# Six full products ahead of a searched run of row-tiled matmuls, with a new table of the run

## The chip, the cores and the metric

One core of a Trainium2 chip runs the whole kernel in one launch. The metric is the device time of one execution in microseconds; the number given for a kernel is the median of its runs. Less is better.

## What is computed

A cross network of six layers over 16,384 rows of 416 features, in bf16:

```python
def reference(x0, ws, bs):
    x = x0
    L = ws.shape[0]
    for l in range(L):
        proj = jnp.einsum('bd,de->be', x, ws[l]) + bs[l]
        x = x0 * proj + x
    return x
```

`x0` is 16384 x 416, `ws` 6 x 416 x 416, `bs` 6 x 416.

## The kernel before

**Tiles.** The batch is cut into 8 groups of 2,048 rows (columns on the chip, since x is held transposed: features on the 128 partitions). A pair (g, l) of group and layer is a job; there are 48. A group's columns are four chunks of 512. The 416 features are three blocks of 128 and a rest of 32. So a job has three output tiles (i = 0, 1, 2) of four chunks each, and a "tail", the 32 output features that are left, for which all four chunks share one bank.

A chunk of an output tile is a sum over 416 inputs, that is three input tiles of 128 (t = 0, 1, 2) and the rest of 32, in one PSUM bank. It can be made in two ways. As *full* products (function `full`, L694), one per input tile, with all 128 rows of the array, and one of 32 rows for the rest. Or as thirteen products of 32 rows each (L1153 for the input tiles, L1157 for the rest): three per row group and one more in the row group that holds the rest. Products in different row groups run side by side, so four of them do what a full one does, but the odd one of the thirteen can be packed with others. Two row groups must not work on the same bank at the same time, so a chunk goes from row group to row group.

**What follows a chunk.** ACT reads the bank, adds the bias and writes `tw` (L595); DVE multiplies a pair of chunks by x0 (L607) and adds x (L615). Tails are made in batches of three (L741 and L729) and evacuated by ACT and DVE (L661, L657, L663, L665). Some tails need their residual rotated by partition quarters, which SP does with DMAs (L487, L488). Outputs are transposed by DMA (L945, L957, and L952 for tails), the tails are spread into the rows by a copy (L980, on POOL, and once, for group 5, on DVE), and the rows are stored (L987, L1003).

**The order.** The first jobs are written out by hand, with full products. From the second tile of job (0, 2) on, `stream` emits 528 chunks as 32-row products only (524 searched ones and four that begin the last output). Their order comes from the string `ORDER`, found by a search beforehand. Each letter takes one chunk (named by its age among those begun) to one row group and runs all its products there; "|" stands for a batch of tails, at which all row groups stop. `replay` steps through the string with a clock of its own: a product takes 20 units (`SLOT`), going to another row group of the same bank costs `FENCE`, a batch of tails costs 60 units per tail and `PHASE`; ACT's reading and the sums of the level below give due times (`READ`, `NEXT`, `BACK`, `SUMS`). `banks` lists when the eight banks are free at the run's start, and `act` when ACT is. The engines don't follow that clock: only the order and the choice of banks are taken from it, and semaphores do the waiting. Instructions on SP, ACT, DVE and POOL are issued in order, each in the order in which `stream` recorded them.

In `replay` before, each of the first four chunks has three products per row group like all others, and the start values are

```python
    free, flight, begun, act = [0] * 4, {}, 0, 156
    banks = [(0, 0), (0, 1), (0, 2), (0, 3), (84, 4), (84, 5), (178, 6), (178, 7)]
```

After the run the last output, group 7's last layer, is made in its natural layout (L1218, evacuated by ACT L1267, multiplied and added by DVE L1273 and L1279, stored by L1286).

Of the kernel before, what the change touches and what calls it, by code (L numbers as in the profile page):

```python
# [5 lines left out]
T32 = 32  # L6
# [15 lines left out]
class Program:  # L22
# [192 lines left out]
ORDER = (  # L215
    "ABCDMBCTZOELBaAjZSIfFiQPVKHYBCcTVIDSJATKBQLWBQXKNALCZQLWBQCbMRLWBITWBQPCZMLWRALSBQLCRIbCRAPeJYWH"
    "N|AWPJQGDQBDWNITCJnQCZTIWBLQWNALWBQXCNIDWZIDWJYTCRbIWBLQBSbINWHAVCTUBOQLBaTARaDQZOLUSBDUORbICJbA"
    "aVTMGBPYBWPIRaHAORDYKBXQKBTIWBDUOZITCZIOTFADeRYPCNIbWQFPK|ABPWAVKPQBCPQVKDAVePQBKfMRaHJAbSIBKTAZ"
    "SLcNHCBQXBSMLBaAOXZQKHMVSDBQOXBMKXAVKDQVKDBMebUJOHAVObIRCLQBSfJ|EODBTAOZACbVcPKFAeXRYGPBYWPRAKPQ"
    "BiLMRGDNACbNAaXNISHBYCTNYCbVISPFAePBUKDVQaDRIOXFAOXBAObVQGLBcCXNAePZIWTFASPBcKPRUGDNAWDNQXCJAbWR"  # L220
    "APSJYDaRUDSJUfOF|ITCRIODJAbSJATJCQDOBPcWJDIeVbQOFXAVODUKBXQKBTIBaLQCZTAOQZLWFPAWNDUCNTUBOTIBaLQN"
    "WALVCQXBOQLBaTINWDIVODUCNXAOJXAWJDUeYBXOIZHSUBTOIBbCMZDWIZTO|EBPWQBOLAVCPQVKfMFSDARWPANXCUNSDIBS"
    "XYBTKAReLMVSbIBKTAhSLYNHCBQXNCMLWBAaPQVKDQBaPBUKjMZSXEBSPAZKPQVHCBQWDMRKXBIWDVAOXJAWfYJTCQZOLEBW"
    "DcRCTMJWbERKP|ABPWQBKPAVCPQVKDANebUBKXQNaHJASXIBKTAhSLYNHCBQXNCMLWBAaXQNKHAZWTMBKDYRKXNAWDNQXBOQ"
    "BObIRWDQBOTICfZAXaRIPFCYPBaUPCMVaLBIWDVQCPRICfJAebJUSPFAaPQVGL|MBDSNAPKBAObRUGLBAeXNYKHVAWTJAKTY"
    "BLCYRWDRIOXBIWPBUOLRAKbBAWPZQCLRYCbNIWTBISPBYKPRAeDQVPKAJXCURCPQJaDIBafQVGPBMaXRIOH|ABTOAZKPQBKD"
    "BUPaAVKbQdCbMRWLEBWTARKPYBWDNQKDZISXBIOTBAOfRYKDZQLWBQKXARKXMBWLBQCPZAWbJQGDQZWPBIWPQBOLAVCPQVKj"
    "MFSDARWPANXCUNSLEBSDYRCTIBafIVOTE|BPWRALOBcDOZQKXBIDVaITCRIbBSYLBSIXNaALVOQDKBQXKBITBaQLVOADOZXA"
    "WJAXSJYDSJYXOFQDZOAXBOQXBOQLBaITVCQDSZMLWBIXSBQLOBIbCZQLCZITWBQLBaITNWALVCUTBSATNaIDJWYTBSPAdOXY"
    "SF|AODVPAKNYXCBQXaJcHORAPaRIHCBUbCRMLWBIWTBQKPVALWRMGDBQCbRMWLBAWbNAKPZUCXQJaPBIWPBcKPVAWLMRCLBQ"  # L230
    "XCRMLWFAWTBQCPZAaPJAWbJMSDZcPCNXYSF|AOTBPAaBYSPJUGDdQODJMbWBIXOdAXKNQHCBQWDMRCbJAaTVIODJAfaUBXSc"
    "NKHAZSXIBLCVYLSNEXCMBWPIBWLAVCXQBOTAdaPUBOLQVaHJAbCMZSLUBSLARKfARWLMBKDYRCPRIbWBQXJOALBaQVCPISXB"
    "ASPYVKHMBCbNQeDJMSXZIP|FCATBaQPBOIDaVIDSJYDSZMXGJTASBjMCNULCVITBeQLNWADaRXMCJDYSBQPaJAbWRAjSJUPG"
    "dQLOBAPSBYPCVIPSBIDSVYDKRAbeJMXGBXMCVIPSBcLORALiNAXOJQDCNUTBOAXBeQPaBYLOVALWdMTGBYfSVMLG|ABWPAVK"
    "PQBCPVQCPJAebVAWLNQaHBYOXBUOLAVKbMRGDBQWDMRKXAJCbQVOLEBaXABOTYVGLMRWDIBSXIBTKAZSLMBKDQZKXARWDQNX"
    "KBISXNADOBcWbBMSXIZGDRYCTZIWPBIWfNQGLB|AWPRAKPBUCPRUKDJAbeJQPWFICXBUPChMLWFAWTBQKPVAWLNQCLBQCbMR"
    "WDJMWDVISPFAObBUCPVQKfNALWBQWLNACbRMLCYJTWARLW|AJTMWDJUCTVICTJWADVaMTBaNIDKVYTOBAfaNQLVGMTCJMSDA"
    "BXa"
)


def replay(tails, events, needs, keep):
# [27 lines left out]
    for letter in ORDER:  # L270
        if letter == "|":
# [13 lines left out]
            for k, (_, b) in enumerate(got):  # L285
# [32 lines left out]
def bass_standalone__cross_network_dcn__recsys_kernel(  # L318
# [8 lines left out]
    NT = 3  # L327
    NJ = 4
# [15 lines left out]
    n = 0  # L344
# [678 lines left out]
    items = []  # L1023
# [85 lines left out]
    def stream(run):  # L1109

        chunks, due = [], []
# [20 lines left out]
        count, seen, natural = {}, {}, {}  # L1132
        for _, r, c, b in plan:
            if r < 0:
                dve[0] = max(dve[0], phases.pop(0)) + PAIR * len(behind_tail) + TAILS
                tails(due.pop(0), corners_last=True, banks=c)
                continue
            if c >= len(chunks):
                n = c - len(chunks)
                (nat_bias if n in natural else nat_row)(0, n, b, True)  # L1140
                natural[n] = b
                continue
            (g, l), i, j = chunks[c]
            if (g, l) not in started:
                start_job(g, l, ahead=False)
            count[c] = count.get(c, 0) + 1
            q, ecols = slice(r * T32, (r + 1) * T32), slice(i * P, (i + 1) * P)
            t = seen[c, r] = seen.get((c, r), -1) + 1
            src, stok = x_src(g, l)
            s3, tok3 = x3_src(g, l)  # L1150
            kw = dict(start=count[c] == 1, stop=count[c] == 4 * NT + 1, tile_position=(r * T32, 0))
            if t < NT:
                add("pe", lambda h, l=l, t=t, j=j, b=b, q=q, ecols=ecols, src=src, kw=kw: h.matmul(  # L1153
                    bank(b), wm[l][q, t, ecols], src(t, j, j + 1)[q, :], **kw),
                    reads=[stok(t, j), wm_tok(l, i)], writes=[("ps", b)], row=r)
            else:
                add("pe", lambda h, l=l, b=b, q=q, ecols=ecols, s3=s3, kw=kw: h.matmul(  # L1157
                    bank(b), w3[l][q, ecols], s3[q, :], **kw),
                    reads=tok3 + [("w3", l, r)], writes=[("ps", b)], row=r)
# [23 lines left out]
    s_lo = items.index(("tile", (0, 2), 1))  # L1183
    for n, it in enumerate(items[:s_lo]):
# [11 lines left out]
        banks = job_banks()  # L1196
# [117 lines left out]
    for kk in range(1, KK):  # L1314
        begun = (1,) if kk == 1 else ()
# [49 lines left out]
```

## Time and profile before

| | |
|---|---|
| median of 3 runs | 464.22 us (464.11 to 464.41) |
| the profiled execution's own time | 464.1 us |
| its span, first to last instruction | 462.3 us |
| granted TensorE clock, mean | 0.999 |
| TensorE (PE) busy | 457.0 us, 99% |
| VectorE (DVE) busy | 403.5 us, 87% |
| ScalarE (ACT) busy | 381.3 us, 82% |
| searched run, first product to last | 40.2 to 446.7 us of the span |

In rows of the profile, "L1153 PE MATMUL ps<-x,wm 32*128 32x512 bf16 x6288 | 372.3, 374 | 0.0" reads: line 1153, TensorE, writes ps from x and wm, weights of 32 rows by 128 columns, moving 32 rows by 512 columns, 6288 of them; 372.3 us in which at least one was running, 374 ns for one on average; 0.0 us in which the engine stood idle just before them. Rows of the timeline begin with start and length in us, both from the span's first instruction; "[0.24 <-ACT tw L595]" is an idle time of the engine and what ended it. A row of the chain of waits has start, length and the piece of work. PEld is TensorE's loading of weights, SPq the DMA queue of SyncE.

### The profile page before, as it was taken

Reading aid. Unit: us, or ns where it says so; the run is one execution under the profiler, and the core shown is the slowest. Engines: PE = TensorE matmul, PEld = TensorE weight load, DVE = VectorE, ACT = ScalarE, POOL = GpSimd, SP = SyncE. Lnnn points to the kernel's source line nnn. Section 1 sums busy time; section 2 is a strip of 40 time slices with the busy share of each in tenths; the row PEclk is TensorE's granted clock in tenths of the full one; section 3 lists DMA queues with packets and bytes.
Section 4 is the critical chain, followed back from the end, with each engine's and each line's share of the span. In section 5 each row is a group of like instructions: output and inputs, shape, how many; then the busy total and the mean of one; then the engine's idle time right before and its main releaser. Section 6 shows DMA issues by size and latency. Waiting matters only on the chain.

```text
span 462.3 us, 17810 instructions
## 1 busy us (share of the span) xinstructions
PE 457.0 (99%) x7985; PEld 262.8 (57%) x7989; DVE 403.5 (87%) x698; ACT 381.3 (82%) x606; POOL 8.1 (2%) x20
## 2 busy tenths in 40 slices
PE   9999999999999999999999999999999999999996
PEld 5344656565655656555665556566555565555552
DVE  2897898988889998898989989898988988989997
ACT  4676889888988889798888979888888888888786
POOL 2000000000000000000000000000000000000010
PEclk9999999999999999999999999999999999999999
DMA  8977869200001859099447955690000088172799
GB/s 226 187 169 123 172 123 169 48 22 12 16 4 41 137 186 188 15 129 225 87 89 127 208 99 101 110 220 19 24 3 4 24 141 294 50 114 64 209 161 315
DMA packets 136160, 53.79 MB, mean 116 GB/s; under 512 B 113674, under 2 KB 134676, under 8 KB 136084
## 3 DMA queue, kind: packets, MB, share of 16 engines
q1 hardware_dynamic: 135928, 52.54, 54.5%
q8 instruction: 62, 1.02, 0.9%
q14 instruction: 14, 0.11, 0.1%
q10 hardware_dynamic: 156, 0.11, 0.1%
HBM read 5.97 MB, written 13.63 MB: 42 GB/s over the span
## 4 chain that ended last, share of the span: by engine, by line
PE 95%; DVE 2%; DMA 1%; ACT 1%; issue 0%; SPq 0%; DVEq 0%
PE ps L1153 74%; PE ps L741 7%; PE ps L1157 6%; PE ps L694 4%; PE ps L688 1%; PE ps L729 1%; DVE x L1279 1%; DVE x L1273 1%; DMA wm<-in_ws_dram 1%; ACT tw L595 1%; PE ps L715 1%; PE ps L839 0%; DVE tw L607 0%; DVE x L615 0%; SPq L784 0%
## 5 line engine op out<-in xcount | busy, mean ns | idle before, releaser
L1153 PE MATMUL ps<-x,wm 32*128 32x512 bf16 x6288 | 372.3, 374 | 0.0
L595 ACT ACTIVATE tw<-ps,bias 128x512 bf16<-128x512 f32 x524 | 327.3, 688 | 47.6 <-PE ps L1153 38.0
L1153 PEld LDWEIGHTS ps<-x,wm 32*128 32x128 bf16 x6288 | 219.2, 92 | 137.5 <-ACT tw L595 3.9
L607 DVE TENSOR_TENSOR tw<-tw,x 128x1024 bf16<-128x1024 bf16 x262 | 177.0, 689 | 40.6 <-ACT tw L595 39.5
L615 DVE TENSOR_TENSOR x<-tw,x 128x1024 bf16<-128x1024 bf16 x262 | 170.8, 687 | 0.3
L1157 PE MATMUL ps<-x,w 32*128 32x512 bf16 x524 | 159.3, 374 | 0.0
L1157 PEld LDWEIGHTS ps<-x,w 32*128 32x128 bf16 x524 | 44.6, 92 | 6.7
L741 PE MATMUL ps<-x,wm 128*32 128x512 bf16 x564 | 33.6, 380 | 0.0
L661 ACT ACTIVATE ts<-ps,bias 128x512 bf16<-128x512 f32 x32 | 20.4, 686 | 13.6 <-PE ps L729 13.6
L559 ACT ACTIVATE tw<-ps,bias 128x1024 bf16<-128x1024 f32 (+1 forms) x22 | 20.4, 1000 | 8.7 <-PE ps L715 7.1
L741 PEld LDWEIGHTS ps<-x,wm 128*32 128x32 bf16 x564 | 13.5, 96 | 18.0 <-ACT tw L595 3.2
L694 PE MATMUL ps<-x,wm 128*128 128x512 bf16 x88 | 20.5, 379 | 0.4 <-issue 0.3
L665 DVE TENSOR_TENSOR x<-ts,x 128x512 bf16<-128x512 bf16 x47 | 18.3, 418 | 0.3
L568 DVE TENSOR_TENSOR tw<-tw,x 128x1024 bf16<-128x1024 bf16 (+1 forms) x21 | 13.2, 637 | 2.0 <-ACT tw L559 1.8
L694 PEld LDWEIGHTS ps<-x,wm 128*128 128x128 bf16 x92 | 8.4, 98 | 10.8 <-issue 1.7
L657 DVE SCALAR_TENSOR_TENSOR ts<-ps,bias,x 128x512 bf16<-128x512 f32 x15 | 11.2, 746 | 3.3 <-PE ps L729 3.3
L573 DVE TENSOR_TENSOR x<-tw,x 128x1024 bf16<-128x1024 bf16 (+1 forms) x21 | 12.6, 633 | 0.0
L663 DVE TENSOR_TENSOR ts<-ts,x 128x512 bf16<-128x512 bf16 x32 | 12.4, 417 | 0.0
L980 POOL COPY ost<-ot 128x512 bf16<-128x512 bf16 x5 | 3.8, 750 | 363.0 <-DMA ot<-x 363.0
L849 DVE COPY x<-ps 128x512 bf16<-128x512 bf16 x6 | 2.4, 421 | 8.0 <-PE ps L839 8.0
L1218 PE MATMUL ps<-wm,x 128*128 128x416 bf16 x48 | 9.3, 340 | 0.0
L1267 ACT ACTIVATE x<-ps 128x416 bf16<-128x416 f32 x16 | 7.7, 528 | 1.5 <-PE ps L1218 1.5
(53 smaller groups left out, 74.5 us busy)
## 6 DMA issues: line engine op xcount, KB each, us to landing
out_dram<-ost SPq DMA_DIRECT2D x6, 1664.0 KB, 7.7
x<-x SPq DMA_DIRECT2D x24, 96.0 KB, 2.1
x<-in_x_dram SPq DMA_DIRECT2D x8, 208.0 KB, 3.6
x<-in_x_dram SPq DMA_DIRECT2D x4, 416.0 KB, 7.4
wm<-in_ws_dram SPq DMA_DIRECT2D x5, 312.0 KB, 3.6
x<-x SPq DMA_DIRECT2D x22, 64.0 KB, 2.3
out_dram<-x SPq DMA_DIRECT2D x3, 416.0 KB, 2.6
out_dram<-ost SPq DMA_DIRECT2D x2, 416.0 KB, 2.9
```

What stands on the lines that cost most here:

```text
L559: add("act", lambda h, a=a, w=w, b0=b0: h.activation(tw[r][:, a * CH:(a + w) * CH], psum[:, b0 * CH:(b0 + w) * CH], ACT_F.Identity, bias=b ...
L568: add("dve", lambda h, a=a, e=e: h.tensor_tensor(tw[r][:, a * CH:e * CH], tw[r][:, a * CH:e * CH], x0s[s0][:, i * GC + a * CH:i * GC + e * ...
L573: add("dve", lambda h, a=a, e=e: h.tensor_tensor(xs[so][:, i * GC + a * CH:i * GC + e * CH], tw[r][:, a * CH:e * CH], src(i, a, e), ALU.ad ...
L595: add("act", lambda h: h.activation(tw[r][:, j * CH:(j + 1) * CH], bank(b), ACT_F.Identity, bias=bias[:, i, l:l + 1], scale=1.0), reads=[( ...
L607: add("dve", lambda h: h.tensor_tensor(tw[r][:, o], tw[r][:, o], x0s[s0][:, c], ALU.mult), reads=[("tw", r, k) for k in both] + [x0_tok(s0 ...
L615: add("dve", lambda h: h.tensor_tensor(paired(xs[so][:, c], "p (k j q) -> p j k q"), paired(tw[r][:, o], "p (j k q) -> p j k q"), paired(s ...
L661: add("act", lambda h: h.activation(ts[r][:, :], bank(b), ACT_F.Identity, bias=bias[:, 3, l:l + 1], scale=1.0), reads=[("ps", b), "bias"], ...
L665: add("dve", lambda h: h.tensor_tensor(x3s[so][:, :], ts[r][:, :], res, ALU.add), reads=[("ts", r)] + rtok, writes=[("x3", so), ("x3", so, ...
L694: add("pe", lambda h, t=t, j=j: h.matmul(bank(banks[j]), wm[l][:, t, ecols], src(t, j, j + 1), start=(first and t == 0), stop=(not first a ...
L741: add("pe", lambda h, t=t, j=j, src=src, l=l, b=b, ro=ro, qo=qo: h.matmul(psum[qo, b * CH:(b + 1) * CH], wm[l][:, t, NT * P:D], src(t, j, ...
L1153: add("pe", lambda h, l=l, t=t, j=j, b=b, q=q, ecols=ecols, src=src, kw=kw: h.matmul(bank(b), wm[l][q, t, ecols], src(t, j, j + 1)[q, :], ...
L1157: add("pe", lambda h, l=l, b=b, q=q, ecols=ecols, s3=s3, kw=kw: h.matmul(bank(b), w3[l][q, ecols], s3[q, :], **kw), reads=tok3 + [("w3", l ...
```

## The change

Six full products of the run's first tile (job (0, 2), i = 1) are put in front of the run. Chunk 0 gets none, chunk 1 the input tile t = 0, chunk 2 t = 0 and 1, chunk 3 all three. In the run these chunks then have only what is left: thirteen products of 32 rows, nine, five and one. `replay` counts them so, its start values for ACT and the banks are set earlier by 120 units (six products of 20), and `ORDER` is a new string throughout. The rest of the kernel's text is the same; its lines lie lower by one to six.

```diff
+AHEAD = (0, 1, 2, 3)
...
 ORDER = (
-    "ABCDMBCTZOELBaAjZSIfFiQPVKHYBCcTVIDSJATKBQLWBQXKNALCZQLWBQCbMRLWBITWBQPCZMLWRALSBQLCRIbCRAPeJYWH"
...
+    "ABCDDCBYXCjZQNeDmcIVjGPQlWDINCbUJCXIROEDNeDUJPGABbQVKMHBWATOVAPKVQDBWAXROYLFCQXZOAPBeUPZSH|MBCTM"
...
-    size = [[3 + (r == tails[c]) if c < n - keep else 2 * (r == tails[c]) for r in range(4)] for c in range(n)]
-    free, flight, begun, act = [0] * 4, {}, 0, 156
-    banks = [(0, 0), (0, 1), (0, 2), (0, 3), (84, 4), (84, 5), (178, 6), (178, 7)]
+    whole = [3 - AHEAD[c] if c < 4 else 3 for c in range(n - keep)]
+    size = [[whole[c] + (r == tails[c]) if c < n - keep else 2 * (r == tails[c]) for r in range(4)] for c in range(n)]
+    free, flight, begun, act = [0] * 4, {}, 0, 36
+    banks = [(0, 0), (0, 1), (0, 2), (0, 3), (0, 4), (0, 5), (58, 6), (58, 7)]
...
-            t = seen[c, r] = seen.get((c, r), -1) + 1
+            ahead = AHEAD[c] if c < NJ else 0
+            t = seen[c, r] = seen.get((c, r), ahead - 1) + 1
+            whole = 4 * (NT - ahead) + 1
...
-            kw = dict(start=count[c] == 1, stop=count[c] == 4 * NT + 1, tile_position=(r * T32, 0))
+            kw = dict(start=count[c] == 1 and not ahead, stop=count[c] == whole, tile_position=(r * T32, 0))
...
-            if count[c] == 4 * NT + 1:
+            if count[c] == whole:
                 evacuate_chunk(g, l, i, j, b, read[c])
...
+    _, (g, l), i = items[s_lo]
+    for t in range(max(AHEAD)):
+        full(g, l, i, ring[:NJ], True, True, chunks=[j for j in range(NJ) if AHEAD[j] > t], ts_=[t])
     bka, left = stream(items[s_lo:])
```

More of the change, by code (lines that the diff above doesn't have):

```diff
@@ L220 @@
[L220 to L234, printed above, removed]
@@ new lines @@
+    "IRWPcFCXQZCPIRWDJQWPEBCTAZSPUJCLAZCXMRaLUBWLAVLSgNXGIRCDUNS|IDJTECRODANCfYVKTMFWDUNCPANaXJQODdAT"
+    "OJUCLURODINCbUBCXQNaLEVCTMBaPUBWLMRCLMhCXMJSDIZSPFACTUBSPIVCLUBCXQNaDIZCXIhTaUNH|ANWTIFCDcCVTMJa"
+    "HAWBXAWRLASdLUOBLcOVDUKNbCVIPSBIDSBYTOVIDKVQDSJMXGBAXSZAPKRUDKNUDWNAXKBQXBOgLRWEPBOUZDICTZUCJTMW"
+    "BLMWREDCRXAeBXYSJPEWRDOQLBCcXZSEN|CDQNWDINDCgRbOUFfSIBbiIRDSIBTKYPVCMLBWIDVSIDRKUDBWQbBObIBWQLZO"
+    "UHRCAXdOQLBKQDRaATJOALCZcDWRIbOFULSBcTNCIDSZIPFCUPBWADZWMTBKYPVCMDVacPRGIbWFA|SPBMCPVAPCVgPCNULa"
@@ new lines @@
+    "BULaBQLWZDQKVbMCVAOTJAaLQBKTBcSLAdTKYVCLMVSDINCXYJSPFAODAZOTBYKDVYSLNAKbBYXKQNDKAhTaUBKTMVGDUNSD"
+    "MJTCIZOTABSPUBOLQVCLMRCDQdWbIFS|PBICTVAPSBcPSZALROUDJOUDKVQDJSAfJCQbVCQLNWALNWcTBKQDRaIPBKUPRCAP"
+    "RAaPBWYLRCYLBSYXJCQLVaMBDaMXhSIPBKUPCVMLBWIDVSAPJCYXJCULZSADReMXJGQDRacPFCXMBWM|RCPISFDQDSJACXdQ"
+    "ObBYOLRAaLRUDKRMXCNIDWJYTOBIPCVAPSJUHCAZDaRMXKFYDCcRXaEJTOAZLOBULCAVPYSBPQCNLQCdLMaBLWZMHSBbMCVM"
+    "|RCPISFDQDCNQaXBQCbRMLWBULhOEDNaQXBKQPCdMLBWIDVSIDRKUDJCQbWBLQOVAfBOULRaEPVCUDROULFCAXRaAPJSUDRK"
@@ new lines @@
+    "UPFCUPBWADZWMTBKYPVCMLBacLROALNaQDJOQDhKQPFCrMBWM|RCPISFDQDSJACXdMSbJUHNCUPBWAPRWAPBOUDNcWLZEODV"
+    "YOTBIOBfUKRDSIPBKAZTKUNHAWBTCYDRWYPJCIXZAWDRMeXYJGPUBWPCMVLBWAPVSDMRKDYBOTYJCLQVaEDVSfMFCUPBWAPV"
+    "SDMRKDYBWTYJOXERCM|RCPISFDADaNQXKFgDSZAbOJUTCJQDSZIPFCUPBWAPVSIDRKUDBOYTJWMDVCMfVKQDSJMDaJATKVAf"
+    "JSUDRKPUFCUPBWMLRCAPBaULNCULZCIXRaMHCNYDWNAPJeQXNCM|CPJUSDJMDCNQaXBMSXdAPKRUHCRMDaNITCBcTNWIDVCM"
+    "TBOYLVSALReAbJOUDVKQPFCYPBWAPVSIDRKUDJCYXJCQDZeQPFWIbNSEDNCDYNSIXFCATBaQPJCcDOdUTFaIPVCIDRaULBSI"
@@ new lines @@
+    "XNCAPRCYPJCULBeUDNeQLZWEPRCMbBOUSLNA|BCTUPBWMDdWIDRKcXZOEDNaUTBKQNDKMfBKATaBQPKZEDVSYPBKUPCVMLBW"
+    "IDVSIDRKUDBWQbBObIBWQLZOALVOAXdKQDJSgDRKUPBKMBbCMRDeMZTGUBTWMJDWIRDKQDBWMfBOUbBWMLZCULZSMDZOAPJW"
+    "QbNCM|CPJUSDJMDWJMCXBMSXdAPKRUHCRMDaNITCBcTNWAPVKQDRKMDBOYTJeMXRCIDVSIPFCUPBWAPVSIDRCYPBOYXJSEDR"
+    "aATZKUBTKUNDWIPBKUDVSAPRKAbBWYLNCYLVOAXJOYHBCUTZeI|NCLUOFDMWDBMCXZMKfRUCLRMWDNAaPJAbKRUODNLUCJDY"
+    "CVMbSBMaDYVKPERCbMRWDINCXYJDWIBXCUNTKAdLQCZLQeNHAaNXCUNL|AWBPUBWPAOZDYOVQCPdaDURObEJCbRWMDNTUOAB"
```

8 lines of the change are left out of this document (1 added, 7 removed).

## The prediction

> **What bounds the kernel now.** I read the page first: busy times, then the chain that ended last, then the costliest groups.
>
> ```profile
> span 462.3 us, 17810 instructions
> PE 457.0 (99%) x7985; PEld 262.8 (57%) x7989; DVE 403.5 (87%) x698; ACT 381.3 (82%) x606; POOL 8.1 (2%) x20
> PE 95%; DVE 2%; DMA 1%; ACT 1%; issue 0%; SPq 0%; DVEq 0%
> L1153 PE MATMUL ps<-x,wm 32*128 32x512 bf16 x6288 | 372.3, 374 | 0.0
> L1157 PE MATMUL ps<-x,w 32*128 32x512 bf16 x524 | 159.3, 374 | 0.0
> L694 PE MATMUL ps<-x,wm 128*128 128x512 bf16 x88 | 20.5, 379 | 0.4 <-issue 0.3
> ```
>
> TensorE is the bound: 95% of the chain, and nothing idle ahead of the two groups that make up the searched run, 6288 + 524 = 6812 products of 32 rows. "Busy" says little here, because four such products run side by side, one in each row group (call it a lane). A lane that stands empty while another works doesn't show as idle. So the question is how full the lanes are, and that I worked out from counts. First the price of a product:
>
> ```profile
> 37.53 2.76 PE L694 MATMUL ps<-x,wm 128*128 128x512 bf16 x12
> 40.23 0.83 PE L1153 MATMUL ps<-x,wm 32*128 32x512 bf16 x12
> 57.18 0.40 PE L1153 MATMUL ps<-x,wm 32*128 32x512 bf16 x3
> 57.51 2.12 PE L741 MATMUL ps<-x,wm 128*32 128x512 bf16 x36
> 59.92 0.85 PE L1153 MATMUL ps<-x,wm 32*128 32x512 bf16 x12
> 86.31 0.41 PE L1153 MATMUL ps<-x,wm 32*128 32x512 bf16 x2
> 446.46 0.59 PE L1153 MATMUL ps<-x,wm 32*128 32x512 bf16 x3
> ```
>
> These are rows of the timeline of TensorE: start, length, instructions merged. Twelve full products take 2.76 us with the last one's 0.379 in it (L694's mean above), so one starts every (2.76 - 0.379)/11 = 0.2165 us. I use the same for a product in its lane. The run's first product starts at 40.23, and its last at 446.46 + 0.59 - 0.374 = 446.68. The first group of tails (L741) ends the lead-in, the second group follows 86.31.
>
> The groups by line, cut to the lead-in and then to the stretch between the first two groups of tails:
>
> ```profile
> L1153 PE MATMUL ps<-x,wm 32*128 32x512 bf16 x288 | 17.3, 375 | 0.0
> L1157 PE MATMUL ps<-x,w 32*128 32x512 bf16 x23 | 7.2, 374 | 0.0
> ...
> L1153 PE MATMUL ps<-x,wm 32*128 32x512 bf16 x454 | 26.8, 374 | 0.0
> L1157 PE MATMUL ps<-x,w 32*128 32x512 bf16 x38 | 11.4, 374 | 0.0
> ```
>
> Lead-in: 288 + 23 = 311 products fill four lanes for 311/4 x 0.2165 = 16.83 us. They took from 40.23 to the last start, 57.18 + 0.40 - 0.374 = 57.21, plus one product: 17.19 us. So 0.36 us of lane time is empty. Next stretch: 492 products fill 26.63 us and took 86.35 + 0.22 - 59.92 = 26.64. That one is full. **The whole emptiness that a better lead-in can remove is therefore about 0.35 us**, 0.08% of the time.
>
> **Part 1, the six full products.** Each full product has the 128 rows that four lane products had. Chunks 0 to 3 lose 0, 4, 8 and 12 lane products, 24 in all; six full ones come in. 24/4 x 0.2165 = 1.30 us removed, 6 x 0.2165 = 1.30 us added: nothing by itself. The order of instructions on TensorE shows them directly behind the twelve full products of the tile before, with the same weights tensor and x tile. Their banks were read by ACT's first pair below, over at 39.54, before the earliest of them could start. Their inputs were already used by that tile. So no wait is added in front, and SP and POOL have nothing here.
>
> ```profile
> 37.42 2.12 ACT L559 ACTIVATE tw<-ps,bias 128x1024 bf16<-128x1024 f32 x2 [1.23 <-PE ps L715]
> 39.90 2.12 ACT L559 ACTIVATE tw<-ps,bias 128x1024 bf16<-128x1024 f32 x2 [0.36 <-PE ps L694]
> 44.22 5.89 ACT L595 ACTIVATE tw<-ps,bias 128x512 bf16<-128x512 f32 x10 [2.20 <-PE ps L1153]
> ```
>
> The pass from full to lane products has a price: the last full one starts at 37.53 + 2.76 - 0.379 = 39.91, the first lane one 0.32 us later, 0.10 more than a product. It is paid once before and once after, six products later. The Trainium skill (TensorEngine Tiling (Array Packing), Key Properties) says that a change of tiling mode drains TensorE, which would speak against full products mixed into a run of lane products. The 0.10 us agrees; by that rule six of them inside the run would have cost a second pair of passes, and here, at its edge, none. I take 0 and keep 0 to +0.10 us.
>
> The run's other four banks come from the second ACT pair, over at 42.02. Moved by 1.30 us the run starts at 41.52, needs the first of these banks about 0.2 us later (that half is read by 40.96) and the last pair about 0.65 us later, at 42.17. That covers 42.02 by 0.15 us; without the cover the one lane that needs it stands, at most 0.1 us. I take 0.
>
> **Part 2, the lead-in.** Before, all four chunks start together, each needs all four lanes, and no bank is complete until late: ACT stands 2.20 us, to 44.22. After, chunk 3 has one lane product left, chunk 2 five, chunk 1 nine, so chunks end one after another and lanes find the next chunk open. How full that makes them is the new table's matter, so I stepped the kernel's own `replay` through both tables and used it only for where each product stands (20 units to a product). Old table against the trace: its tails end at 1,822 units, and 59.92 - 40.23 = 19.69 us is 0.01081 us per unit; its last product starts at 37,618, and 446.68 - 40.23 = 406.45 us is 0.01080. The trace keeps the table to a hundredth of a percent, so a unit is 0.0108 us.
>
> Empty lane units up to the first tails: 134 in the old table, 12 in the new. That is 122/4 = 30.5 units, **-0.33 us**, just under the 0.35 us that the rows allow.
>
> **Part 3, the rest of the new table.** All other empty places (fences between lanes of a bank, uneven ends) are 338 lane units in the old table and 380 in the new: 42/4 = 10.5 units, **+0.11 us**. In sum the new run ends at 37,498 + 120 (the six) = 37,618 units against 37,638: -20 units, **-0.22 us**. Unknown here is only what the table doesn't model. It knows lanes, banks and sums of one level down; it doesn't know tails' DMAs or DVE's turns. In the old order these never delayed TensorE.
>
> **Part 4, the end.** After the run the chain is ACT and DVE:
>
> ```profile
> 444.23 0.05 PE ps L1153
> 444.28 0.02 issue
> 444.30 3.01 ACT tw L595 x5
> 447.31 0.02 issue
> 447.34 0.69 DVE tw L607
> 448.03 1.20 DVE x L615 x2
> ```
>
> Five evictions in a row hang on chunk ends shortly before the run's end, so a shift of the run passes on whole only if the last chunks keep their spacing. The last four end 120, 60, 16 and 0 units before the end in the old table, 104, 60, 18 and 0 in the new. The fifth eviction (0.60 us each) then ends 0.20 to 0.26 us earlier than before, and all behind it is the same list of instructions. I take -0.22.
>
> **Part 5, what moves on the other queues.** From the second group of tails on, tails come 30 to 295 units (0.3 to 3.2 us) later against the tiles. On SP two rotations of a tail residual, four DMAs, are now behind a load:
>
> ```profile
> 273.88 0.54 SPq L487 DMA_DIRECT2D x<-x  x1
> 276.78 5.18 SPq L438 DMA_TRANSPOSE ost<-in_x_dram  x4
> 282.01 5.70 SPq L427 DMA_TRANSPOSE x<-in_x_dram  x4
> 287.75 3.29 SPq L462 DMA_DIRECT2D x<-ost  x4
> 292.31 0.50 SPq L487 DMA_DIRECT2D x<-x  x1
> ```
>
> In the old order they go out at 273.88 ahead of 276.78; behind the load and its own rotation they go out near 291 and land by 295 (from 273.88 to 276.78 four of them take 2.9). The next tails in the new order end near 40.23 + 24,376 x 0.0108 = 303, and their residual isn't read earlier. 8 us cover it; I take 0. The one move with little cover is the first rival.
>
> **Sum** on the profiled execution (464.1 us, span 462.3, 1.8 around it, unchanged): 0 - 0.33 + 0.11 = -0.22, so 463.9. The median, 464.22, lies 0.12 above the profiled one: **464.0 us**. The likeliest case's own range is 463.8 to 464.2. One per mille is less than the 0.2% (0.93 us) that a measurement of this kernel can tell from no change.
>
> **Rival A, a DVE copy now meets its DMA: slower.** These are DVE's and SP's rows where group 5's tails are turned for output:
>
> ```profile
> 420.96 0.75 DVE L665 TENSOR_TENSOR x<-ts,x 128x512 bf16<-128x512 bf16 x2
> 421.40 1.19 SPq L952 DMA_TRANSPOSE ot<-x  x1
> 422.55 0.69 DVE L607 TENSOR_TENSOR tw<-tw,x 128x1024 bf16<-128x1024 bf16 x1 [0.23 <-ACT tw L595]
> 425.57 1.28 DVE L615 TENSOR_TENSOR x<-tw,x 128x1024 bf16<-128x1024 bf16 x2
> 426.77 0.28 DVE L980 COPY ost<-ot 128x512 bf16<-128x512 bf16 x1
> 432.41 1.29 DVE L607 TENSOR_TENSOR tw<-tw,x 128x1024 bf16<-128x1024 bf16 x2 [0.55 <-ACT tw L595]
> DMA to landing us min/median/max: 2.4/2.4/2.4
> DMA to landing us min/median/max: 2.4/2.6/4.4
> ```
>
> The copy L980 needs the transpose L952, issued at 421.40 as soon as the first L665 is done and landed 2.4 us later, at 423.8; it ran at 426.77 with 2.97 to spare. Between L665 and the copy stand eight additions and multiplications. In the new order of DVE there are four, because the tails come later. Four at 0.60 and the 0.23 idle go: the copy's turn is near 424.1, 0.3 us after the landing. Should the transpose take the 4.4 us that is the longest of its seven, the copy holds DVE for 1.7 us. Behind it stand the sums that TensorE's next level reads. DVE's gaps of 0.23 and 0.55 us there swallow some; the rest, up to 1.4 us, TensorE waits: 464.0 + 1.4 = 465.4. It decides against the change from a landing of about 3.2 us (0.45 us held, 0.22 passed on), and passes 0.2% only above 4 us. For it: two of seven landings were over 3.5. Against: at this place it was 2.4, and SP's queue is as empty.
>
> **Rival B, the whole emptiness goes: faster by over 0.2%.** All empty lane time of the old run is 472/4 = 118 units, 1.27 us; without it the time is 462.95. Against: the new table still has 392.
>
> **Rival C, no gain.** The exchange 24 for 6 is even, and if the gain at the lead-in is lost (a late bank in lane order, another 0.10 us pass), the time is 464.1 to 464.3. The new table's few empty places speak against it.
>
> **Rival D, TensorE waits somewhere unmodelled in the new order** (a bank released late, once in each of 15 groups of tails, 0.1 us each): +1.5 - 0.22, 465.5. Against: the old order, made under the same fences, showed no such sum in 406 us.
>
> **How the numbers follow.** Forecast 0.62; C 0.15; A 0.12, of which 0.04 above 465.15; B 0.04; D 0.07. Faster by over 0.2%: B and 0.01 for what I don't see, 0.05. Slower: A's 0.04, D's 0.06, together 0.10. Within: 0.85. The range must leave out no more than 0.2: 463.6 (the forecast with all of the lead-in's 0.33 kept, and another 0.3 of emptiness gone) to 464.8 (A with a landing of 3.8 us: 1.07 held, 0.84 passed on).
>
> **What would show it.** Right: the first 32-row product near 41.5, six more L694 in front of it; ACT's 2.20 us wait gone; tails at about 40.23 + 1,504 x 0.0108 = 56.5 and the second at 86.9; last run product at about 446.5. Wrong: an idle time on DVE ahead of the copy, of over 0.5 us (A); lanes of later stretches emptier than 0.1 us each (D); a run that ends before 446 (B).

## The result and the profile after

The changed kernel takes 464.83 us (median of 13 runs, 464.41 to 466.14). The kernel before took 464.22 us beside it (13 runs, 463.78 to 464.93). The ratio is 1.0017, with a 95% interval of 1.0010 to 1.0025: slower by about 0.6 us where 0.2 us less were forecast. That is still inside 0.2%, but clear of zero.

The page of the profile after, with the lines that answer to those of before:

```profile
span 464.3 us, 17775 instructions
PE 458.0 (99%) x7971; PEld 260.8 (56%) x7971; DVE 404.1 (87%) x698; ACT 380.4 (82%) x606; POOL 7.8 (2%) x20
PE 95%; DVE 3%; ACT 1%; issue 0%; DVEq 0%
L1156 PE MATMUL ps<-x,wm 32*128 32x512 bf16 x6264 | 371.1, 374 | 0.0
L1160 PE MATMUL ps<-x,w 32*128 32x512 bf16 x524 | 154.4, 374 | 0.0
L695 PE MATMUL ps<-x,wm 128*128 128x512 bf16 x98 | 22.8, 383 | 0.0
```

24 products of 32 rows are gone (6288 to 6264). DVE's share of the chain rose from 2% to 3%. This profiled execution took 466.14 us, the longest of the thirteen, so its span can't be set against that of before. I compare stretches instead, each counted from the run's first or last product. What lies ahead of the run is the same code. Without the six products (1.30 us) it ends at 40.49 to 41.21 us in the 13 profiles of the new table below, and at 40.15 to 41.41 in the 7 of the old one, so it shifts by up to 1.3 us from profile to profile and shows no loss of its own.

TensorE's timeline after (start, length, instructions merged):

```profile
37.80 4.06 PE L695 MATMUL ps<-x,wm 128*128 128x512 bf16 x18
41.78 0.39 PE L1156 MATMUL ps<-x,wm 32*128 32x512 bf16 x3
56.51 0.41 PE L1156 MATMUL ps<-x,wm 32*128 32x512 bf16 x3
56.84 2.13 PE L742 MATMUL ps<-x,wm 128*32 128x512 bf16 x36
87.25 2.13 PE L742 MATMUL ps<-x,wm 128*32 128x512 bf16 x36
447.00 0.37 PE L1156 MATMUL ps<-x,wm 32*128 32x512 bf16 x1
```

The groups by line in the lead-in after, and ACT's row that had the 2.20 us wait:

```profile
L1156 PE MATMUL ps<-x,wm 32*128 32x512 bf16 x253 | 15.1, 375 | 0.0
L1160 PE MATMUL ps<-x,w 32*128 32x512 bf16 x23 | 6.9, 375 | 0.0
```

```profile
44.39 4.54 ACT L596 ACTIVATE tw<-ps,bias 128x512 bf16<-128x512 f32 x7 [1.47 <-PE ps L1156]
```

**The lead-in did what was forecast.** 276 products fill 276/4 x 0.2165 = 14.94 us of four lanes. They took from 41.78 to the last start, 56.51 + 0.41 - 0.37, plus one product: 14.98 us. So 0.04 us is empty where 0.36 was.

**The run lost more than that behind it.** The run goes from 41.78 to 447.00, 405.22 us. The table's end, 140 units earlier than before without the six products, says 406.45 - 140 x 0.0108 = 404.94. So 0.28 us is lost here, and with the six products (1.30 us) the run takes 406.52 instead of 406.45. Two more profiles of the same kernel gave 405.27 and 405.34.

The first place is the tenth group of tails. DVE's rows there (L608 multiplies and L616 adds for the tiles, L658 reads the tails' bank):

```profile
300.57 0.69 DVE L608 TENSOR_TENSOR tw<-tw,x 128x1024 bf16<-128x1024 bf16 x1
301.29 0.98 DVE L616 TENSOR_TENSOR x<-tw,x 128x1024 bf16<-128x1024 bf16 x1
302.19 1.28 DVE L608 TENSOR_TENSOR tw<-tw,x 128x1024 bf16<-128x1024 bf16 x2
303.39 1.28 DVE L616 TENSOR_TENSOR x<-tw,x 128x1024 bf16<-128x1024 bf16 x2
304.60 0.74 DVE L658 SCALAR_TENSOR_TENSOR ts<-ps,bias,x 128x512 bf16<-128x512 f32 x1
```

ACT, GpSimd and TensorE's loading of weights in the same stretch:

```profile
304.00 1.26 ACT L662 ACTIVATE ts<-ps,bias 128x512 bf16<-128x512 f32 x2 [1.18 <-PE ps L730]
```

```profile
300.81 0.91 POOL L981 COPY ost<-ot 128x512 bf16<-128x512 bf16 x1 [46.18 <-DMA ot<-x]
```

```profile
305.39 0.10 PEld L1156 LDWEIGHTS ps<-x,wm 32*128 32x128 bf16 x3 [0.48 <-DVE ts L658]
```

ACT reads the first banks of these tails at 304.00. DVE's reading comes 0.60 us later, behind the multiplications and additions that stand ahead of it in its order, and TensorE's next weights wait for it. One addition takes 0.98 instead of 0.69 us, and a copy of GpSimd runs beside it. In the old order such a copy ran at 299.01 and no multiplication or addition there was longer than 0.69. The Trainium skill (SBUF — State Buffer, Who interferes with whom) says that a VectorE instruction with two SBUF inputs contends with a GpSimd instruction that reads SBUF, over ports that one of them holds as an exclusive lock. The trace agrees that the two get in each other's way; waiting out the rest of the copy as the profile shows it (from 301.29 to 301.72) would be an estimated 0.43 us, where 0.29 was lost.

The second place is behind the run. DVE, GpSimd and SP after:

```profile
447.55 0.69 DVE L608 TENSOR_TENSOR tw<-tw,x 128x1024 bf16<-128x1024 bf16 x1 [0.29 <-ACT tw L596]
448.16 1.48 DVE L616 TENSOR_TENSOR x<-tw,x 128x1024 bf16<-128x1024 bf16 x2
```

```profile
447.24 1.27 POOL L997 COPY ost<-ot 128x256 bf16<-128x256 bf16 x2 [23.28 <-DMA ot<-x]
```

```profile
441.00 3.60 SPq L958 DMA_TRANSPOSE ost<-x  x2
444.64 1.28 SPq L953 DMA_TRANSPOSE ot<-x  x1
```

The rows of the kernel before that answer to the last three:

```profile
443.60 1.72 POOL L996 COPY ost<-ot 128x256 bf16<-128x256 bf16 x2 [22.73 <-DMA ot<-x]
```

```profile
439.78 2.04 SPq L952 DMA_TRANSPOSE ot<-x  x1
441.91 5.38 SPq L957 DMA_TRANSPOSE ost<-x  x4
```

The last tails are about 2 us later against the run's end. Their transpose (L953) therefore goes out behind two of the lanes' transposes (L958) instead of ahead of them, GpSimd's two copies move from 443.60 to 447.24, and they meet the two additions at 448.16, which take 1.48 instead of 1.29. From the run's last product to DVE's last end it is 13.43 us instead of 13.36.

The third place is the end of the transfers, read in a profile nearer to the median (after_again below, 465.26 us). The DMA view of its last 20 us, in slices of 0.5 us from 446, then issues (operation, count, KB each, median us to landing):

```profile
GB/s 183 3 160 210 163 204 207 157 216 197 249 396 251 198 92 20 142 373 396 409 426 396 403 409 396 409 423 413 419 376 393 351 92 0 0 0 0 0 0 0
out_dram<-x SPq DMA_DIRECT2D x3, 416.0 KB, 3.5
out_dram<-x SPq DMA_DIRECT2D x1, 104.0 KB, 2.2
```

The same view of the kernel before:

```profile
GB/s 217 204 184 161 13 9 241 263 204 351 376 252 212 201 362 379 413 353 370 379 376 356 386 416 406 399 406 330 263 220 207 0 0 0 0 0 0 0 0 0
out_dram<-x SPq DMA_DIRECT2D x3, 416.0 KB, 2.6
out_dram<-x SPq DMA_DIRECT2D x1, 104.0 KB, 1.7
```

Before, the rate falls from some 400 to 207 GB/s in the last 2 us: the transfers have caught up, and the last stores wait for DVE. After, the rate stays near 400 to the end: DVE is done and the transfers are still behind. From DVE's last end to the end of the span it is 2.72 us here, and 2.23 before.

### The profile page after: what moved, and what is told of

Its sections match the earlier page's. It is cut to its first block, busy times and chain, and to the rows that moved or that the text cites. A ratio compares the mean times of both kernels' runs of the same rounds, so it can differ in the third digit from the quotient of the medians.

```text
span 464.3 us, 17775 instructions
## 1 busy us (share of the span) xinstructions
PE 458.0 (99%) x7971; PEld 260.8 (56%) x7971; DVE 404.1 (87%) x698; ACT 380.4 (82%) x606; POOL 7.8 (2%) x20
## 4 chain that ended last, share of the span: by engine, by line
PE 95%; DVE 3%; ACT 1%; issue 0%; DVEq 0%
PE ps L1156 73%; PE ps L742 7%; PE ps L1160 6%; PE ps L695 5%; PE ps L689 1%; PE ps L730 1%; DVE x L1279 1%; DVE x L1285 1%; PE ps L822 1%; ACT tw L596 1%; PE ps L840 1%; PE ps L716 1%; DVE x L616 0%; DVE tw L608 0%; DVE x L1247 0%
## 5 line engine op out<-in xcount | busy, mean ns | idle before, releaser
L1156 PEld LDWEIGHTS ps<-x,wm 32*128 32x128 bf16 x6264 | 216.9, 92 | 139.0 <-ACT tw L596 5.0
L608 DVE TENSOR_TENSOR tw<-tw,x 128x1024 bf16<-128x1024 bf16 x262 | 177.2, 691 | 41.4 <-ACT tw L596 40.1
L616 DVE TENSOR_TENSOR x<-tw,x 128x1024 bf16<-128x1024 bf16 x262 | 171.7, 690 | 0.5
L1160 PE MATMUL ps<-x,w 32*128 32x512 bf16 x524 | 154.4, 374 | 0.0
L1160 PEld LDWEIGHTS ps<-x,w 32*128 32x128 bf16 x524 | 43.4, 92 | 6.1 <-issue 0.2
L695 PE MATMUL ps<-x,wm 128*128 128x512 bf16 x98 | 22.8, 383 | 0.0
L569 DVE TENSOR_TENSOR tw<-tw,x 128x1024 bf16<-128x1024 bf16 (+1 forms) x21 | 13.2, 638 | 1.9 <-ACT tw L560 1.8
L658 DVE SCALAR_TENSOR_TENSOR ts<-ps,bias,x 128x512 bf16<-128x512 f32 x15 | 11.2, 748 | 1.9 <-PE ps L730 1.9
L981 POOL COPY ost<-ot 128x512 bf16<-128x512 bf16 x5 | 3.9, 785 | 364.0 <-DMA ot<-x 364.0
```

The lines of the kernel that those rows point to most:

```text
L569: add("dve", lambda h, a=a, e=e: h.tensor_tensor(tw[r][:, a * CH:e * CH], tw[r][:, a * CH:e * CH], x0s[s0][:, i * GC + a * CH:i * GC + e * ...
L608: add("dve", lambda h: h.tensor_tensor(tw[r][:, o], tw[r][:, o], x0s[s0][:, c], ALU.mult), reads=[("tw", r, k) for k in both] + [x0_tok(s0 ...
L616: add("dve", lambda h: h.tensor_tensor(paired(xs[so][:, c], "p (k j q) -> p j k q"), paired(tw[r][:, o], "p (j k q) -> p j k q"), paired(s ...
L695: add("pe", lambda h, t=t, j=j: h.matmul(bank(banks[j]), wm[l][:, t, ecols], src(t, j, j + 1), start=(first and t == 0), stop=(not first a ...
```

## The experiments

A ratio is that of the times to the kernel before on the same chip, with its 95% interval. "Run" is from the run's first product to its last; "DVE end" from the run's last product to DVE's last end; "end" from there to the end of the span. The theories, as they were named: 1, the end is held by its DMAs, group 5's late store above all; 2, TensorE waits in the new order; 3, it is scatter only; 4, the end's DMAs hold both kernels alike and the first profile of before was lucky; 5, later tails bring GpSimd's copies onto DVE's close turns.

**Is it real, and is it group 5's store?** That store of 1664 KB was issued at 427.08 and landed at 434.17 before, just ahead of the end's transposes at 434.33. After, it was issued at 429.50 and landed at 437.94. (One expectation below gives it 832 KB, which is the size of group 6's last store.) after_again is the changed kernel unchanged.

> The changed kernel once more, as the control of this set. Its first profile ended with output DMAs that landed 3.0 to 3.9 us after their issue (1.7 to 1.9 before) and with 0.28 us of TensorE waits in the run. Theory 1 (the end is held by DMAs: group 5's store goes out 2.4 us later and runs into the transposes from 434.5 on): about 464.8, and the last stores of this profile too land later than 2 us after issue. Theory 2 (waits of TensorE in the new order, the end only follows): the run takes 405.2 us or more from first to last product, and the last stores land within 2 us. Theory 3 (scatter of the executions only): 464.0 to 464.3.

after_store_first puts the four rotations that stand ahead of that store behind it:

```diff
...
+                if (LAST - 2, L - 1) in batch:
+                    put_off.append((g, l + 1))
+                    continue
                 prefill(g, l + 1)
...
             store(LAST - 2, 0, NJ)
+            while put_off:
+                prefill(*put_off.pop(0))
```

> The changed kernel, but the four rotation DMAs of the fourteenth batch of tails are issued behind group 5's store instead of ahead of it, so that the store goes out right after its copy, near 427.5 instead of 429.5, and lands near 435.5. Theory 1: 0.3 to 0.7 us less than the control, 464.1 to 464.5. Theory 2: as the control within 0.1 us.

before_late_store delays the store in the old table, by a tile:

```diff
...
-            store(LAST - 2, 0, NJ)
+        elif (g, l, i) == (LAST - 1, L - 2, 1):
+            so = xset[(g, l + 1)]
+            store(LAST - 2, 0, NJ, [("x", so, i, j) for j in range(NJ)])
```

> The kernel before, with one more wait: group 5's store also waits for the sums of the next tile of job (6, 4), so that it goes out near 429.5 instead of 427.1, as in the changed kernel; nothing else differs, the table is the old one. Theory 1: slower than the kernel before by 0.3 to 1.0 us, about 464.8, with last stores that land 3 us or more after issue. Theory 2: 464.2, as before.

after_no_store5 leaves the store out.

> The changed kernel without group 5's store (1664 KB): those rows of the output are not written. Theory 1: the end is free of it and the forecast of the table comes out, 464.0 to 464.2. Theory 2: as the control, 464.8.

| kernel | us | ratio | run | DVE end | end |
|---|---|---|---|---|---|
| before, first profile | 464.22 | | 406.45 | 13.36 | 2.23 |
| after_again | 465.42 | 1.0015 (1.0006 to 1.0024) | 405.27 | 13.42 | 2.72 |
| after_store_first | 465.22 | 1.0010 (1.0001 to 1.0019) | 405.22 | 13.42 | 2.68 |
| before_late_store | 465.30 | 1.0012 (1.0003 to 1.0021) | 406.48 | 13.36 | 2.77 |
| after_no_store5 | 465.22 | 1.0011 (1.0002 to 1.0020) | 405.22 | 13.42 | 2.53 |

The loss is real. A late store alone can cost as much: before_late_store has the old run and the old DVE end, and lost 0.6 us, with an end of 2.77. But in the new table neither an earlier store (landed at 435.25) nor none brought the time back. So Theory 1 was right that the end counts and too narrow in its cause.

**How much is the end, and how much TensorE?** before_again is the kernel before. after_no_store6b and before_no_store6b leave out the last 832 KB store of group 6 (half of that group's output isn't written), so that the last stores find the way free. after_tail10 makes DVE read the bank of the tenth tails ahead of the additions that stood in front:

```diff
-            if behind_tail or phases and max(dve[0], ready[(g, l, i, a)]) + PAIR > phases[0] + 14:
+            if behind_tail or phases and max(dve[0], ready[(g, l, i, a)]) + PAIR > phases[0] + (14 if len(phases) != 6 else -100):
```

> The kernel before once more, for a second profile of it: one look. If the end of the kernel before is held by DVE (its first profile: last stores landed 1.7 us after issue, 2.2 us from DVE's last instruction to the end), these two numbers come again. If the end's DMAs are as crowded in it (theory 4: the end is the same in both kernels and the first profile of before was a lucky one), the last stores land 2 us or more after issue and 2.5 us or more follow DVE's last instruction.

> The changed kernel with one turn on DVE changed: at the tenth batch of tails the second of the two pairs of sums ahead of it goes behind DVE's reading of the tails' bank. In four profiles of the changed kernel TensorE stood still there by 0.17 to 0.22 us, since DVE read that bank 0.6 us after it was complete. Theory 2 (waits of TensorE in the new order): first to last product of the run takes 405.05 us instead of 405.22 to 405.27, and the time falls by 0.1 to 0.25 us against the changed kernel. Theory 1 (the end's DMAs set the time): the run gets shorter in the same way, but of it less than half arrives at the end.

> The changed kernel without the last store of group 6 (832 KB, half of its rows are not written), the transfer in front of the last stores on their queue. Theory 1 (the end is held by DMAs): the last stores land within 2 us, 2.2 us from DVE's last instruction to the end, and the time falls by 0.4 us or more against the changed kernel, to about 0.1 us over the kernel before. Theory 2: as the changed kernel within 0.15 us.

> The kernel before without the same store. Theory 1: its end isn't held by DMAs, so it gains 0.15 us or less. Theory 4 (the end's DMAs hold both kernels alike): it gains as much as the changed kernel does from the same cut, 0.3 us or more.

| kernel | us | ratio | run | DVE end | end |
|---|---|---|---|---|---|
| before_again | 464.20, one run | | 406.45 | 13.36 | 2.44 |
| after_tail10 | 464.96 | 1.0013 (1.0003 to 1.0022) | 405.03 | 13.43 | 2.57 |
| after_no_store6b | 464.63 | 0.9999 (0.9990 to 1.0008) | 405.35 | 13.43 | 2.24 |
| before_no_store6b | 464.35 | 0.9998 (0.9990 to 1.0007) | 406.47 | 13.36 | 2.23 |

Without that store the changed kernel's end is 2.24 and it is level with the kernel before; the old table gains nothing from it (0.9998). So the end of the transfers carries most of the loss. Between the last two, 0.28 us remains by the medians; the two profiles show 0.18 of it in the run with the six products (405.35 + 1.30 against 406.47) and 0.07 in DVE's end. Theory 4 was partly right: an end of 2.44 occurs in the old table too. after_tail10 took 0.2 us out of the run with one changed place in DVE's order, so it was DVE's late reading that held TensorE; the time, 0.0013, still did not show it beyond its interval.

**What slowed DVE?** after_third is the changed kernel again. after_no_pool and before_no_pool leave out GpSimd's copies L981 behind the first group and the two at the end (L997), so that 32 columns of most groups' output aren't right. after_mended is after_tail10, and besides holds the lanes' transposes until the last tails' own transpose is out, as in the old order:

```diff
...
+        if g not in rested:
+            waiting.append((g, i, a, a + 2))
+            return
...
                 turn_rest(g)
+                rested.add(g)
+                while waiting:
+                    turn_out(*waiting.pop(0))
```

> The changed kernel a third time, as the control of this set: 0.5 to 0.8 us over the kernel before; run 405.2 to 405.35 us from first to last product; 13.42 us from the last product's start to the end of DVE's last instruction; two of DVE's last additions (L616) together 1.48 us instead of 1.29.

> The changed kernel without POOL's copies that spread the tails into the output rows, but for group 0's (32 columns of the other groups but one are not right). In every profile of the changed kernel a POOL copy runs at 301 while DVE's addition takes 0.98 instead of 0.69 us and DVE comes late to the tails' bank, and two POOL copies run at 447 to 449 while DVE's last additions take 1.48 instead of 1.29. Theory 5 (the later tails bring POOL's copies onto DVE's close turns): both additions come back to 0.69 and 1.29, the run takes 405.05 to 405.1, from the last product to DVE's end 13.2 to 13.25, and the time falls by 0.3 to 0.4 us against the control. Rival (the additions are slowed by DMA traffic at these places): both stay as they are.

> The kernel before without the same copies. Theory 5: its copies lie where DVE has time, so run (406.45) and DVE's end (13.36) stay and the time is 464.4, as before within 0.15 us. Rival (POOL's copies cost both kernels alike): it gains as much as the changed kernel.

> The changed kernel with two turns put back: DVE's order at the tenth tails, and on SP the transpose of group 6's tails ahead of the two transposes of its rows, as in the kernel before. All output is made. Theory 5 (with the end's DMAs behind it): POOL's last copies end before 446.5, DVE's last additions take 1.29, run 405.05, last product to DVE's end 13.2 to 13.3, time 0.3 to 0.6 us less than the control, level with the kernel before within 0.2 us. If the end's DMAs are late for another reason, the run and DVE's end get shorter and the time doesn't follow.

| kernel | us | ratio | run | DVE end | end |
|---|---|---|---|---|---|
| after_third | 465.61 | 1.0020 (1.0011 to 1.0028) | 405.34 | 13.43 | 2.69 |
| after_no_pool | 464.91 | 1.0010 (1.0000 to 1.0019) | 405.03 | 13.36 | 4.03 |
| before_no_pool | 464.62 | 1.0002 (0.9993 to 1.0010) | 406.45 | 13.36 | 2.38 |
| after_mended | 465.52 | 1.0016 (1.0004 to 1.0029) | 405.03 | 13.36 | 2.60 |

(The profiled execution of after_no_pool took 466.37 us; its end of 4.03 is that of a late one, like the 3.90 of the changed kernel's first profile, 466.14 us.) DVE's rows in after_third, where GpSimd's copy ran from 302.08 for 0.93 us:

```profile
301.85 0.69 DVE L616 TENSOR_TENSOR x<-tw,x 128x1024 bf16<-128x1024 bf16 x1
302.46 1.70 DVE L608 TENSOR_TENSOR tw<-tw,x 128x1024 bf16<-128x1024 bf16 x2
```

The same two in after_no_pool, and its pair at the end:

```profile
301.61 0.69 DVE L616 TENSOR_TENSOR x<-tw,x 128x1024 bf16<-128x1024 bf16 x1
302.22 1.28 DVE L608 TENSOR_TENSOR tw<-tw,x 128x1024 bf16<-128x1024 bf16 x2
448.30 1.29 DVE L616 TENSOR_TENSOR x<-tw,x 128x1024 bf16<-128x1024 bf16 x2
```

What is slow moves with the copy from profile to profile (one addition of 0.98 in after, two multiplications of 1.70 in after_third) and is gone with it. The run then is 405.03, 0.1 us over what the table says (404.94), and DVE's end 13.36 as in the kernel before (13.2 to 13.25 had been expected), while the old table gains nothing. That is Theory 5, shown for the run and for DVE's end. The time is less clear: the median is 0.7 us under the control's where 0.3 to 0.4 had been expected, and the two intervals overlap. In after_mended, with all output made, the copies are early again. GpSimd's and DVE's rows:

```profile
444.70 1.20 POOL L1004 COPY ost<-ot 128x256 bf16<-128x256 bf16 x2 [20.66 <-DMA ot<-x]
```

```profile
448.30 1.28 DVE L617 TENSOR_TENSOR x<-tw,x 128x1024 bf16<-128x1024 bf16 x2
```

Run and DVE's end fell by 0.38 us together against after_third, but the time did not follow: its twelve runs lie between 464.41 and 466.88. The transfers hold it.

**What holds the transfers?** after_mended_store_first is after_mended with the rotations behind group 5's store as in after_store_first; after_mended_no_store5 and before_no_store5 leave that store out.

> The kernel of after_mended (the run's stall and the end's additions are already as short as before in its profile), in which, besides, the tile rotations of the fourteenth tails are issued behind group 5's store. All output is made. If group 5's late store is what keeps the end's transfers late: the store is issued near 427 and lands before 435.5, the transposes of the end start behind it, the last six landings take 2 us or less after DVE's last instruction's store, and the time comes out at or below the kernel before (464.2 to 464.7, ratio 0.998 to 1.0005), as the run with its six products is 0.1 us shorter than the run of before. If the store is only one of several loads on the end's queue: as after_mended, 465.1 to 465.6, ratio 1.001 to 1.0020.

> The kernel of after_mended without the 832 KB store of group 5's lanes, so that part of the output is not written. If that store's time is the cause: 464.0 to 464.6, level with the kernel before or under it. If the end's transfers are late for another reason that came with the new table: 465.0 to 465.5, ratio above 1.0008.

> The kernel before without the same store, as the control. In its profile the store lands at 434.17, ahead of the end's transposes at 434.33, so by the theory of the store its absence changes nothing: ratio 0.999 to 1.0006. If the end's queue is loaded by this store in the old table too, 0.2 us or more under the kernel before (ratio under 0.9995).

after_one_out is after_mended_store_first with one of the lanes' transposes let through ahead of the last tails' one, so that SP doesn't stand:

```diff
...
-        if g not in rested:
+        if g not in rested and g in one_out:
             waiting.append((g, i, a, a + 2))
             return
+        one_out.add(g)
```

> after_mended_store_first with one transpose of the last lanes (out of six) issued ahead of the last tails' own transpose, so that the end's transposes on SP's queue follow each other without the hole of 0.98 us that stands there in after_mended's trace (SP idle from 440.53 to 441.51). All output is made. If that hole is what keeps the last transposes late: the last of them lands 7.0 to 7.3 us after the run's last product starts (before 7.02, after_mended_store_first 7.87), the last landings take 1.7 to 2.0 us, the end after DVE is 2.2 to 2.4 us, and the time is at or below the kernel before (464.3 to 464.8, ratio 0.998 to 1.0003). If the hole is no cause, the last transposes land 7.8 us behind as now, the end after DVE is 2.6 to 2.7 us and the ratio is 1.0003 to 1.0015.

after_mended_no_store6b is after_mended without group 6's last store; before_no_store6b_again is its partner on the same chip.

> after_mended without the last 832 KB store of the six lanes' results, so that half of that group's output is not written. This leaves the new table's run and DVE's end, mended, without the crowded end of the transfers. If the three places add up: run with its six products 0.12 us shorter than the run of before, DVE's end at 13.36, end after DVE 2.23, so 0.1 us under before_no_store6b_again (ratio to the kernel before 0.9985 to 0.9998). If the mended order costs something besides, it comes out above that kernel (ratio over 1.0000).

> The kernel before without the same store, once more, on the chip of the two others. As before_no_store6b: ratio 0.9990 to 1.0005, end after DVE 2.23 us.

| kernel | us | ratio | run | DVE end | end |
|---|---|---|---|---|---|
| after_mended_store_first | 465.11 | 1.0006 (0.9998 to 1.0015) | 405.04 | 13.37 | 2.69 |
| after_mended_no_store5 | 465.03 | 1.0007 (0.9995 to 1.0018) | 405.04 | 13.36 | 2.63 |
| before_no_store5 | 464.71 | 0.9997 (0.9988 to 1.0007) | 406.47 | 13.36 | 2.23 |
| after_one_out | 465.26 | 1.0012 (1.0003 to 1.0021) | 405.05 | 13.36 | 2.80 |
| after_mended_no_store6b | 464.46 | 0.9998 (0.9989 to 1.0007) | 405.03 | 13.36 | 2.25 |
| before_no_store6b_again | 464.74 | 1.0000 (0.9990 to 1.0010) | 406.45 | 13.36 | 2.24 |

The last pair came out as expected: with the crowd at the end gone, the mended table is 0.28 us under the old one by the medians (0.12 by the two profiles, 405.03 + 1.30 against 406.45), though within the intervals. before_no_store5 changed nothing (0.9997), as was expected of it if the store weighs nothing in the old table. Group 5's store and the hole on SP's queue fell as the cause: no version with all its output came out below the kernel before. after_mended_store_first is the nearest, and can't be told from it.

Set side by side, the profiles show what the end hangs on. Counted from the run's last product, these are the landing of the last transpose (L957 or L958), and of the last store:

| kernel | last transpose landed | last store landed | difference |
|---|---|---|---|
| before | 7.03 | 15.11 | 8.08 |
| before_no_store5 | 7.21 | 15.11 | 7.90 |
| before_again | 7.67 | 15.31 | 7.64 |
| before_late_store | 7.97 | 15.64 | 7.67 |
| after_mended | 7.76 | 15.49 | 7.73 |
| after_mended_no_store5 | 7.78 | 15.51 | 7.73 |
| after_mended_store_first | 7.87 | 15.58 | 7.71 |
| after_one_out | 7.96 | 15.69 | 7.73 |
| after_third | 7.96 | 15.64 | 7.68 |
| after_again | 7.98 | 15.66 | 7.68 |

Group 6's last store, 832 KB, needs the last transpose; the rest of the last layer's stores follow it, two of 416 KB that each land 1.05 us behind the one before, then 208 KB and two of 104 KB. That chain is 7.7 us long. DVE's own chain ends at 13.36 + 0.03 and its last store lands 1.72 us behind, at 15.11. So the transfers set the end once the last transpose lands later than 7.4. The old table lies on both sides of this edge, every profile of the new one beyond it. Why the last transpose lands later in the new table is not settled. It is issued at about the same time (3.91 before, 3.80 to 4.00 in the six profiles of the new table that stand above); its landing takes 3.1 us before and 3.7 in before_again, and 3.9 to 4.2 us in those six. In the two late ends, after and after_no_pool, it was issued at 5.23 and 5.28 and landed at 9.03 and 9.10. Group 5's store and the order of the end's transposes were tried, and neither is the cause alone. What was not tried is a table with the lead-in of the new one and the last two groups of tails where the old one has them.

The profiles do show one thing that moved. The DMA queue that they name "instruction" carries 62 packets of 16 KB in each of the 20 profiles. The last of them as the DMA view has it (packets, MB, share of the 16 engines), before from 447.2 to 448.4 and in after_again from 451.5 to 452.5:

```profile
q8 instruction: 1, 0.02, 5.5%
q8 instruction: 1, 0.02, 5.8%
```

Counted from the run's last product it starts at 0.61 to 1.60 us in the seven profiles of the old table (1.16 on average) and at 3.08 to 4.21 in the thirteen of the new one (3.72), and it takes 0.93 to 1.72 us. Of the last six lanes' transposes in all 20 profiles, the 61 that had no such packet between issue and landing took 3.12 to 3.82 us, and every one that took longer, up to 5.40, had one. In the old table the last packet meets some of the third to fifth of the six and never the sixth. In the new one it meets the fifth and sixth, or in the two late ends the fourth and fifth, and little time is left to catch up. That makes it the likeliest reason, but no run moved this packet alone, so it is not shown.

## Why the prediction was wrong

**What bounds the kernel** held: TensorE has 95% of the chain in both profiles, and the empty lead-in was worth about a third of a microsecond.

**Part 1** (six full products, 0): right. From the first full product to the first lane product it was 40.23 - 37.53 = 2.70 us before and 41.78 - 37.80 = 3.98 after, 1.28 more against 1.30. From the last full product's start (37.80 + 4.06 - 0.38 = 41.48) to the lane product is 0.30 us, as before (0.32). The banks' cover held.

**Part 2** (lead-in, -0.33): right; the emptiness fell from 0.36 to 0.04 us.

**Part 3** (rest of the table, +0.11, and "it doesn't know tails' DMAs or DVE's turns. In the old order these never delayed TensorE") is the step that failed first. What the old order never showed was carried over to a new one. The run with its six products was forecast at 406.24 us, took 406.52 to 406.64 in the first three profiles, and 406.33 once DVE's reading of the tenth tails was put ahead or GpSimd's copies left out. So 0.2 to 0.3 us is the wait that the table doesn't model, and 0.1 us small ones that I didn't trace.

**Part 4** (the end passes on -0.22 whole, "all behind it is the same list of instructions") failed next, and by more. ACT's part was right, even a little better: from the last product's start to DVE's next multiplication 0.55 us after, 0.66 before. But the same list had other neighbours: GpSimd's copies lengthened two additions by 0.19, which made +0.07 of it. And the list didn't cover the transfers. I took the 2.23 us behind DVE as fixed, when it stood at the edge where the transfers take over; they added 0.25 to 0.49 us (2.69 and 2.72 against 2.23 and 2.44). Why the last transpose came in past that edge in every profile of the new table stays open.

**Part 5** (rotations on SP, 0) was right at the place I named: they went out from 291.56 and the residual was read at 304.60. It stopped one place too early. The same lateness of the tails put group 5's store from 427.08 to 429.50 and the last tails' transpose behind others, and there SP's queue had no 8 us of cover; but neither of these, put back (after_store_first, after_mended), brought the time back by itself.

**The sum**: forecast -0.22. By the profiles the run gives +0.12 to +0.19 (after_again and after_third), DVE's end +0.07, the transfers +0.25 to +0.49: +0.4 to +0.75, around the 0.6 of the medians. The time, 464.83, lies just above the range's 464.8.

**Rivals.** A did not occur: the transpose L953 was issued at 424.49 and landed in 2.45 us, and DVE's copy ran at 427.11 without idle time, 0.17 us behind the landing. The rival had looked at the right lateness and priced the wrong victim. Its two landings over 3.5 us, of seven, took 4.40 and 3.77; those two alone had a packet of the instruction queue between issue and landing. B did not. C's "no gain" is near the run's outcome, but by losses behind the lead-in and not in it. D named the kind, "TensorE waits somewhere unmodelled", and was priced as 15 waits of 0.1 us; there was one of 0.2 to 0.3 us. The rival that was missing is the end of the transfers.

**What would show it**: the first 32-row product at 41.78 (41.5 forecast, with a head 0.27 us later) and tails at 56.84 and 87.25 (56.5 and 86.9) agree with this shift. ACT's 2.20 us wait was to be gone, and 1.47 us of it stayed. The run's last product at 447.00 instead of 446.5 shows the loss behind.

## What to carry to other kernels

A model that has matched one order to a hundredth of a percent has only shown that what it leaves out was hidden in that order; for a new order, list what it leaves out (copies of other engines, reads by a shared engine, stores) and look where each now falls. When a step makes some work later, follow its stores to the end of the kernel: the cover that counts is that of the last transfers, and it may be used up although the engine's chain shows the end as its own. Before costing the stretch behind the last instruction at a constant, see whether the transfer rate falls off there; if it stays at its highest to the end, there is nothing left to hide behind.

## What the runs showed of the hardware that was not expected

- A bf16 addition of two 128x1024 operands on VectorE took 0.98 instead of 0.69 us beside a GpSimd copy of 128x512, two multiplications of the same size took 1.70 instead of 1.28 in another profile, and two additions 1.48 instead of 1.29 beside two copies of 128x256. Without those copies each was back at its short time.
- Which of them is hit differs between profiles of one kernel, as the copy starts when its DMA lands (300.81 in after, 302.08 in after_third). The one that was already running when the copy began (at 300.57 in after, at 301.85 in after_third) kept its 0.69 us.
- The last stores move at about 400 GB/s: two of 416 KB, 1.05 us apart.
- The last six transposes (L957 or L958) landed 3.12 to 3.82 us after issue when no 16 KB packet of the queue named "instruction" ran in between; with one in between they took 3.26 to 5.40 us. That the packet is the reason, no run shows.
